# Top-32 attention feeding a squared-ReLU MLP: weights cast by GpSimd DMAs, a reordered first load, and identity products on TensorE

## The chip, the cores and the metric

The kernel runs on one NeuronCore of a Trainium2 chip. The core's engines are TensorE (PE, with its weight loads shown as PEld), VectorE (DVE), ScalarE (ACT), GpSimd (POOL) and SyncE (SP, which here only issues DMAs). The metric is the device time of one execution in microseconds, as the median of several runs. One further execution was taken with the hardware profiler; it has its own time and its own span, from the first instruction to the last.

## The reference

Attention in which each query keeps only its 32 largest scores, followed by a two-layer MLP with a squared ReLU. q, k and v are 8 batches x 8 heads x 576 rows x 64, in fp32.

```python
scores = scale * np.matmul(q, k.transpose(0, 1, 3, 2))
kth = np.partition(scores, -top_k, axis=-1)[..., -top_k:-top_k + 1]
scores = np.where(scores >= kth, scores, -1000000000.0)
attn = softmax(scores)                       # over the last axis
x = np.matmul(attn, v)                       # -> (4608, 512), heads side by side
h = x @ w_in                                 # w_in  512 x 2048, fp32
r = np.maximum(h, 0.0)
out = (r * r) @ w_out                        # w_out 2048 x 512, fp32
```

## The kernel before

**Groups.** The work is cut into 144 groups, 18 for each batch: a group is 128 query rows of two heads (a "pair" of heads shares one load), or, for the last 64 rows of a head (`Z`), 64 rows of four heads. In batches 0 to 6 the order is first row blocks 0 and 1 of each pair, then blocks 2 and 3 with the `Z` groups between them; in the last batch it is `Z`, then blocks 2 and 3, then block 0 of all pairs and block 1 of all pairs.

**One group.** `top_k` (L519) makes the scores on PE: eight fp32 matmuls into `ps_s`, three PSUM banks of which there is one set only. ACT copies them to SBUF (`s`, L555). DVE forms maxima of halves (`pairs`, L611, which read `ps_s` and so release it for the next scores); one of the two goes to a PSUM bank `ps_q`, and ACT copies it into `m` (L619). DVE combines the two (L621), and POOL forms the lower values by whole-number additions and subtractions (L606). Then DVE takes eight maxima at a time and strikes them out: MAX8 (L638) and MATCH_REPLACE8 (L642) on 104, 124 and 272 columns for each of the two halves, and one MAX8 over all 576 (`kth`, L645). The strikes wait for POOL's operation `mid`. ACT makes the mask term `w` from scores and threshold (L653).

`attend` (L669) transposes the scores on PE and adds the mask with a product by `steep_bf`; the ninth block of it uses the bank `ps_q` too. ACT takes the exponential into `p` (L687). `collect` multiplies by v, ACT copies the result (`av`, L714), DVE takes reciprocals (L716), POOL scales (`x`, L718), PE transposes and ACT copies into `xt` or `xz` (L742, L743). When all heads of 256 rows are there, `feed` (L748) runs the MLP on that chunk: products with `win`, ReLU on ACT (L768), square on POOL or ACT (L782, L785; on DVE for the last chunk, L779), products with `wo`, a copy (`o`, L802) and the store (L810).

**Loads.** `load_pair` (L459) issues three DMAs for q (`rq`), three for k (`rk`) and five for v (`rv`); the first pair's k goes out on ACT's queue, everything else on SP's. PE transposes q and k through `ident32`, ACT copies them into `qk` (L511 to L514), POOL casts v (L515).

**Weights.** `setup` (L856) makes the identities and constants on POOL, and then brings in the two weight matrices in 16 pieces of 0.5 MB of fp32: a DMA on SP's queue into one of two staging buffers `ws`, which lie in the last slots of the MLP's own buffer `g`, and a cast into `win` or `wo` on ACT or POOL (L894). The pieces with `i % 4` of 0 or 1 go to ACT, eight in all, and the others to POOL.

```python
pl.op("sp", 4.0, WD * i - 60, lambda ...: [nc.sync.dma_start(view(s), src)],
      w=[s], take=[s], ndma=1, sem=..., nbf=WN)
eng, fn = ("act", act.copy) if i % 4 < WA else ("gp", gp.tensor_copy)
weights.append(pl.op(eng, 1.1, WC * i, lambda ...: fn(dst, view(s)), r=[s]))
```

**What sets the order.** Nothing is ordered by hand. Each operation is given to a `Plan` with an engine, an estimated duration and a priority (smaller goes first), and `Plan.schedule` (L120) plays the program through with these durations: at each moment an idle engine takes its ready operation of the smallest priority whose buffers are free. An operation is not ready before its `nbf` time. The order that comes out is emitted for each engine and is fixed: at run time every engine works in that order, waiting on semaphores. Priorities are due times: group n (from 0) has `tg = T0 + PER * n` with `T0 = 12.0` and `PER = 5.55`. Named constants shift them: `LEAD` (scores), `ME` and `MQ` (the pair operations and their combination), `MA`, `MP`, `TW` (mask), `TA`, `TL` and `NL` (`attend`, with an extra lead that grows over the last `NL` groups up to `TL`), `LAG`, `STEP` and, for the last batch, `LAGL` (`feed`).

Of the kernel before, what the change touches and what calls it, by code (L numbers as in the profile page):

```python
# [8 lines left out]
FP32 = mybir.dt.float32  # L9
# [3 lines left out]
P = 128  # L13
# [63 lines left out]
class Op:  # L77
    __slots__ = ("eng", "dur", "prio", "fn", "deps", "tiles", "takes", "n", "users", "start", "end",
                 "idx", "sem", "val", "ndma", "seq", "vc", "waits", "wars", "later", "nbf", "lk", "late",
                 "via")  # L80
# [5 lines left out]
class Plan:  # L86
# [3 lines left out]
    def op(self, eng, dur, prio, fn, r=(), w=(), u=(), hold=(), take=(), after=(), order=(), sem=None, ndma=0, nbf=0.0, lk=False, late=0.0, via=None):  # L90
# [6 lines left out]
        o.sem, o.ndma, o.seq, o.nbf, o.lk, o.late, o.via = sem, ndma, len(self.ops), nbf, lk, late, via  # L97
# [22 lines left out]
    def schedule(self, t0=0.0, latency=0.12, own=0.07):  # L120
# [24 lines left out]
        while events:  # L145
# [19 lines left out]
            for e in ENGS:  # L165
# [3 lines left out]
                while ready[e]:  # L169
# [23 lines left out]
                    hold = o.dur if e != "sp" else 0.6 * o.ndma  # L193
                    o.end = o.start + o.dur + (hold if e == "sp" else 0)
# [15 lines left out]
class Emitter:  # L210
# [9 lines left out]
    def number(self, plan):  # L220
        for e in ENGS:
            for o in plan.order[e]:
                if e == "sp":
# [12 lines left out]
        seq = sorted(plan.ops, key=lambda o: (o.start, 0 if o.eng != "sp" else 1, o.seq))  # L236
# [41 lines left out]
    def emit(self, plan, e, eng):  # L278
        for o in plan.order[e]:
# [5 lines left out]
            if e == "sp":  # L285
                for i in ins:
                    i.then_inc(self.sem(o.idx[0]), 16)
            else:
                ins.then_inc(self.sems[e], 1)


def bass_top_k_attn__then__act_relu_squared_kernel(
# [22 lines left out]
    def sb(name, shape, dt=FP32, n=None):  # L315
# [7 lines left out]
    ME = 16.41  # L323
    MQ = 15.52
    MP = 18.0
    MA = 18.98
    SQ = 5.15
    TA = 7.2
    TW = -0.14
    TL = 8.0  # L330
    NL = 28.07
    WD = 3.33
    WC = 1.75
    WA = 1.13
    WN = 6
    NBO = 3.81
    LAG = 11.28
    STEP = 3.19
    LATE = 2.38
    LAGL = 11.07  # L340
# [21 lines left out]
        "rq": ([P, 5, 2, D], FP32, 2), "rk": ([P, 5, 2, D], FP32, 2), "rv": ([P, 12, D], FP32, 2),  # L362
# [9 lines left out]

# [3 lines left out]
    NWS = 2  # L376
    mem["ws"] = [gmem[:, NG - 4 - 4 * i:NG - 4 * i, :].rearrange("p a c -> p (a c)").bitcast(FP32) for i in range(NWS)]
    pools["g"], pools["ws"] = Pool("g", NG), Pool("ws", NWS)
# [70 lines left out]
    first_h = []  # L449

    def build(full, weights, pl):
# [6 lines left out]

        def load_pair(b, hp, base):  # L459
# [3 lines left out]
            def load(t, src, rest, queue=nc.sync):  # L463
                def fn():
                    r = at(t)
                    res = []
                    for h in range(2):
                        r0 = 64 if h and rest != (512, 512) else 0
                        res.append(queue.dma_start(r[:, 0:4, h, :], src[b, 2 * hp + h, r0:r0 + 512, :].rearrange(
                            "(tb p) d -> p tb d", p=P)))  # L470
                    x = src[b, 2 * hp, rest[0]:rest[0] + 64, :]
                    res.append(queue.dma_start(r[0:64, 4, :, :], bass.AP(
# [13 lines left out]
            pl.op("sp", 2.3, base - 80, load(rq, q, (512, 512)), w=[rq], take=[rq], sem=slot_sem, ndma=3)  # L486
            via = "act" if not full and not state["pairs"] else None
# [260 lines left out]
        def feed(chunk, xt, tm, step):  # L748
# [7 lines left out]
            for i, g in enumerate(gs):  # L756
# [18 lines left out]
                if chunk in FIRST and weights:  # L775
                    first_h.append(ho)
# [224 lines left out]
```

## Time and profile before

| | |
|---|---|
| median of 3 runs | 872.97 us (872.86 to 874.77) |
| the profiled execution: time | 870.8 us |
| the profiled execution: span | 869.0 us |
| DVE busy | 822.5 us (95%) |
| PE busy | 809.9 us (93%) |
| POOL busy | 788.2 us (91%) |
| ACT busy | 760.3 us (87%) |
| moved by DMA | 48.21 MB, mean 55 GB/s |
| first DVE instruction | 12.51 us |
| last cast of weights | 71.81 us |

The page gives busy times over the whole span and a row of 40 slices for each engine, where a digit is the busy share in tenths. A table of stages gives the same for stretches that the reader picks. The view of waits says for each group of instructions what the engine stood idle for, in total, how often, and the longest. The timeline lists instructions in order of time, with the idle time just ahead of them and what ended it in brackets. A matmul's end is modelled, so a busy PE is not a PE at its peak rate.

### The profile page before, as it was taken

To read this page: it belongs to the slowest core of one execution; us is meant where nothing else is said; L and a number is where in the kernel's file an instruction comes from. 1 tells how busy PE (TensorE), PEld (TensorE's weight loads), DVE (VectorE), ACT (ScalarE), POOL (GpSimd) and SP (SyncE) were. 2 spreads that over 40 slices of the span, in tenths; PEclk is the share of its full clock that TensorE was granted. 3 is DMA by queue.
4 is the path that set the end of the run, shared out by engine and by line. 5 is a ranking of instruction groups with operands and counts; after the bars stand their busy time and mean duration, and the time that the engine had idled before them with its cause. 6 is when DMAs were issued, how large, how long until landed. Compare 5 with 4: busy or idle time off the path is not lost.

```text
span 869.0 us, 22447 instructions
## 1 busy us (share of the span) xinstructions
PE 809.9 (93%) x7911; PEld 612.7 (71%) x7970; DVE 822.5 (95%) x3413; ACT 760.3 (87%) x1261; POOL 788.2 (91%) x826
## 2 busy tenths in 40 slices
PE   5777999989999999998999999999999999999996
PEld 3555777757687777766878677777777767677784
DVE  2989999999999999999999999999999999999971
ACT  4787998989898899989989799889999889898973
POOL 6898999999999998999999889998999987999971
PEclk9899999999999999999999999999999999999999
DMA  7881212131210223012131022202121021100000
GB/s 176 210 231 49 56 29 69 28 85 26 55 43 14 67 56 77 21 38 58 29 87 26 25 60 59 74 13 56 44 68 42 14 52 43 41 2 14 26 25 31
DMA packets 126969, 48.21 MB, mean 55 GB/s; under 512 B 119168, under 2 KB 119168, under 8 KB 126848
## 3 DMA queue, kind: packets, MB, share of 16 engines
q1 hardware_dynamic: 125648, 46.39, 21.3%
q8 instruction: 65, 1.06, 0.5%
q14 instruction: 56, 0.46, 0.2%
q10 hardware_dynamic: 1200, 0.30, 0.2%
HBM read 37.22 MB, written 9.44 MB: 54 GB/s over the span
## 4 chain that ended last, share of the span: by engine, by line
DVE 64%; PE 17%; ACT 11%; issue 4%; POOL 1%; DMA 1%; SPq 0%; DVEq 0%
DVE f L642 21%; DVE c L638 16%; PE ps L444 13%; DVE kth L645 13%; DVE f L621 5%; PE ps L447 5%; DVE ps L611 5%; DVE m L611 4%; ACT s L555 3%; ACT p L687 3%; ACT w L653 1%; ACT g L768 1%; POOL f L606 1%; POOL t L606 1%; DVE rzall L716 1%
## 5 line engine op out<-in xcount | busy, mean ns | idle before, releaser
L642 DVE MATCH_REPLACE8 f<-c,f 128x104 f32<-128x104 f32 (+2 forms) x864 | 272.2, 325 | 0.0
L638 DVE MAX8 c<-f 128x8 f32<-128x104 f32 (+2 forms) x864 | 248.8, 329 | 0.0
L447 PE MATMUL ps<-ident,s 128*128 128x128 f32 x1296 | 223.1, 281 | 21.5 <-ACT p L687 14.7
L653 ACT ACTIVATE w<-s,kth 128x576 bf16<-128x576 f32 x288 | 222.8, 786 | 19.8 <-DVE kth L645 18.5
L444 PE MATMUL ps<-qk 64*128 64x64 f32 (+3 forms) x1280 | 214.2, 454 | 10.2 <-DVE m L611 8.8
L606 POOL TENSOR_TENSOR t<-s 128x576 int32<-128x576 int32 x144 | 202.5, 1411 | 13.2 <-ACT s L555 13.1
L645 DVE MAX8 kth<-f 128x8 f32<-128x576 f32 x288 | 209.5, 757 | 0.0
L606 POOL TENSOR_TENSOR f<-t,m 128x576 int32<-128x576 int32 x144 | 203.2, 1411 | 0.1
L444 PEld LDWEIGHTS ps<-qk 64*128 64x128 f32 (+1 forms) x1280 | 132.6, 181 | 86.6 <-issue 62.9
L555 ACT COPY s<-ps 128x1152 f32<-128x1152 f32 x144 | 161.5, 1121 | 34.7 <-PE ps L444 33.7
L447 PEld LDWEIGHTS ps<-ident,s 128*128 128x128 f32 x1296 | 144.3, 142 | 48.0 <-ACT p L687 23.6
L687 ACT ACTIVATE p<-ps 128x1152 bf16<-128x1152 f32 x144 | 163.3, 1134 | 8.7 <-PE ps L444 7.8
L444 PE MATMUL ps<-steep_bf,w 128*128 128x128 bf16 x1296 | 141.1, 220 | 0.0
L606 POOL TENSOR_TENSOR t<-m 128x288 int32<-128x288 int32 x144 | 115.0, 799 | 19.3 <-ACT m L619 14.7
L444 PE MATMUL ps<-wo,g 128*128 128x512 bf16 x517 | 127.9, 379 | 4.0 <-issue 1.1
L444 PE MATMUL ps<-xt,win 128*128 128x256 bf16 (+1 forms) x1152 | 126.6, 261 | 1.5 <-ACT qk L511 0.8
L606 POOL TENSOR_TENSOR f<-t,f 128x288 int32<-128x288 int32 x144 | 114.9, 798 | 0.0
L444 PEld LDWEIGHTS ps<-xt,win 128*128 128x128 bf16 x1152 | 97.9, 98 | 15.9 <-ACT g L768 1.2
L444 PEld LDWEIGHTS ps<-steep_bf,w 128*128 128x128 bf16 x1296 | 106.0, 101 | 4.2
L782 POOL TENSOR_TENSOR g<-g 128x512 bf16<-128x512 bf16 x92 | 95.7, 1042 | 12.9 <-ACT g L768 11.7
L768 ACT ACTIVATE g<-ps 128x512 bf16<-128x512 f32 x144 | 86.0, 606 | 10.1 <-PE ps L444 9.3
L611 DVE TENSOR_TENSOR ps<-ps,s 128x288 f32<-128x288 f32 x144 | 66.6, 462 | 22.1 <-ACT s L555 17.1
(60 smaller groups left out, 882.4 us busy)
## 6 DMA issues: line engine op xcount, KB each, us to landing
rq<-in_q_dram SPq DMA_DIRECT2D x64, 128.0 KB, 2.5
rv<-in_v_dram SPq DMA_DIRECT2D x64, 128.0 KB, 2.4
out_dram<-o SPq DMA_DIRECT2D x32, 256.0 KB, 2.1
rk<-in_k_dram SPq DMA_DIRECT2D x62, 128.0 KB, 2.6
g<-in_moe_w_in_dram SPq DMA_DIRECT2D x8, 512.0 KB, 4.3
g<-in_moe_w_out_dram SPq DMA_DIRECT2D x8, 512.0 KB, 4.3
rv<-in_v_dram SPq DMA_DIRECT2D x96, 16.0 KB, 2.1
rq<-in_q_dram SPq DMA_DIRECT2D x32, 32.0 KB, 2.5
```

The costliest lines, as they stand in the source:

```text
L444: return pe.matmul(o, l, r, start=start, stop=stop, skip_group_check=True)
L447: return pe.matmul(o, i, ident, is_transpose=True, skip_group_check=True, **kw)
L555: cp = [pl.op("act", 1.2, tg - LEAD + 1, lambda: act.copy(at(st)[:, :, :], two(banks(ss), SECOND, S)), r=[ss], w=[st])]
L606: return pl.op("gp", dur, prio, lambda: gp.tensor_tensor(o().bitcast(I32), x().bitcast(I32), y().bitcast(I32), op), **kw)
L611: return vec.tensor_tensor(o, two(banks(ss)[:, a:], SECOND + HALF, QUART), two(at(st)[:, 0, HALF + a:], HALF, QUART), ALU.max)
L638: lambda i=i, t=t, c0=c0, c1=c1: vec.max(eighth(t, i), at(f)[:, i, c0:c1]),
L642: lambda i=i, t=t, c0=c0, c1=c1: vec.match_replace(at(f)[:, i, c0:c1], eighth(t, i), at(f)[:, i, c0:c1], NEG), hold=[f])]
L645: ks.append(chain(kth, i, prev[i] + [low], .665, lambda i=i: vec.max(eighth(kth, i), at(f)[:, i, :]), hold=[f]))
L653: pl.op("act", .77, tw + .8 * i, lambda i=i: act.activation(at(wt)[:, i, :], at(st)[:, i, :], ACTF.Relu, bias=kth[:, i, n:n + 1], scale=-1.0),
L687: pl.op("act", 1.15, tt + 1, lambda: act.activation(at(pt)[:, :, :].rearrange("p k q -> p (k q)"), banks(e)[:, 0:2 * S], ACTF.Exp, scale=0 ...
L768: return act.activation(at(g)[:, 0:kf * nt], bank(hh)[:, 0:kf * nt], ACTF.Relu)
L782: pl.op("gp", .15 + w_ / 480, tf + lag + 1, lambda g=g: gp.tensor_tensor(at(g)[:, 0:w_], at(g)[:, 0:w_], at(g)[:, 0:w_], ALU.mult), u=[g])
```

## The change

Four things change.

- **Weights.** The staging buffers and the 16 casts go. Eight DMAs of 1 MB of fp32 are issued by POOL and write bf16 straight into `win` and `wo`. They have a high priority on POOL and are not ready before `6 + 6.19 * i` us in the plan. `feed` waits for pieces of the new size.
- **The first pair.** k of the first head goes out on ACT's queue and k of the second on SP's; of q only the first 128 rows of both heads are loaded next, and the rest after that, into a third `rq` buffer. PE transposes the first block of q and all of k, DVE (not ACT) copies most of k into `qk`, and the rest of q is transposed and copied after the first group's scores have been planned.
- **Identity products.** PE gets products of `ident_bf` with itself, 128x512 into a PSUM bank, whose results nobody reads: 36 of them 0.22 us apart in the plan from 0 to 8 us, and 51 more 1.2 us apart up to 70 us. Their priority is the lowest, so that the plan puts them where PE has nothing else that is ready; each takes one of the two `psum` buffers.
- **The plan's constants and its model of DMAs** (a `bw` term holds the queue for the time that a load takes).

```diff
@@ Plan.schedule
-                    hold = o.dur if e != "sp" else 0.6 * o.ndma
-                    o.end = o.start + o.dur + (hold if e == "sp" else 0)
+                    hold = o.dur if e != "sp" else max(o.bw, 0.6 * o.ndma * (o.via is None))
+                    o.end = o.start + o.dur + (hold if e == "sp" else o.bw)
@@ constants
-    ME = 16.41
-    MQ = 15.52
+    ME = 21.85
+    MQ = 19.61
-    MA = 18.98
-    SQ = 5.15
+    MA = 18.27
+    SQ = 5.7
-    TW = -0.14
-    TL = 8.0
-    NL = 28.07
-    WD = 3.33
+    TW = -1.88
+    TL = 19.68
+    WARM = 8
+    WP = 6.19
+    BW = 1
+    WSTEP = 1.2
+    WEND = 70
+    NL = 6.65
-    LAG = 11.28
-    STEP = 3.19
-    LATE = 2.38
-    LAGL = 11.07
+    LAG = 12.79
+    STEP = 2.98
+    LATE = 1.39
+    LAGL = 20.8
@@ buffers
-        "rq": ([P, 5, 2, D], FP32, 2), ...
+        "rq": ([P, 5, 2, D], FP32, 3), ...
-    NWS = 2
-    mem["ws"] = [gmem[:, NG - 4 - 4 * i:NG - 4 * i, :]... for i in range(NWS)]
@@ build
+        def load_first(b, hp, rq, rq2, rk, base):
...
+            pl.op("sp", .1, base - 82, start(nc.scalar, lambda: part(rk, k, 0, 0, 4),
+                                             lambda: rest(rk, k, REST[0], REST[1] - REST[0])),
+                  w=[rk], take=[rk], sem=slot_sem, ndma=2, via="act")
+            pl.op("sp", 2.3, base - 81, start(nc.sync, lambda: part(rk, k, 1, 0, 4)), w=[rk], sem=lambda o: "first", ndma=1)
+            pl.op("sp", 2.3, base - 80, start(nc.sync, lambda: (at(rq)[:, 0, :, :], both)), w=[rq], take=[rq],
+                  sem=slot_sem, ndma=1)
+            pl.op("sp", 2.3, base - 79, start(
+                nc.sync, lambda: part(rq2, q, 0, 1, 3), lambda: part(rq2, q, 1, 1, 3), lambda: rest(rq2, q, 512, 0)),
+                w=[rq2], take=[rq2], sem=slot_sem, ndma=3)
+
+        def first_pair(rq, rq2, rk, rv, qk, vb, base):
...
+            o_x = pl.op("pe", .15, base - 45.2, flips(tx, rq, [0]), r=[rq], w=[tx], take=[tx, qk])
+            o_k = pl.op("pe", .5, base - 45.1, flips(tk, rk, [0, 1, 2, 3]), r=[rk], w=[tk], take=[tk], order=[o_x])
...
+            pl.op("act", .3, base - 42.5, lambda: act.copy(at(qk)[:, 0:128], bank(tx)[:, 0:128]), r=[tx], w=[qk])
+            pl.op("dve", .6, base - 42.5, lambda: vec.tensor_copy(at(qk)[:, 640:1152], bank(tk)), r=[tk], w=[qk])
...
@@ setup
-        for i in range(16):
-            s = tile("ws")
...
-            weights.append(pl.op(eng, 1.1, WC * i, lambda s=s, dst=dst, view=view, fn=fn: fn(dst, view(s)), r=[s]))
+        for i in range(8):
+            if i < 4:
+                half, c2 = divmod(i, 2)
+                src = wi[:, 2 * c2:2 * c2 + 2, 1024 * half:1024 * half + 1024]
+                dst = win[:, 2 * c2:2 * c2 + 2, 1024 * half:1024 * half + 1024]
+            else:
+                src, dst = wo_ap[:, 4 * i - 16:4 * i - 12, :], wo[:, 4 * i - 16:4 * i - 12, :]
+            weights.append(pl.op("gp", 1.0, WC * i - 60, lambda src=src, dst=dst: [gp.dma_start(dst, src)], ndma=1,
+                                 sem=lambda o, i=i: f"w{i}", nbf=WN + WP * i, bw=7.0))
+
+        times = [.22 * i for i in range(int(WARM / .22))]
+        times += [WARM + WSTEP * i for i in range(int((WEND - WARM) / WSTEP))]
+        for x in times:
+            t = Tile(psum)
+            pl.op("pe", .22, 1e5, lambda t=t: mm(bank(t), ident_bf[:, :], ident_bf[:, :].unsqueeze(1).broadcast_to(
+                [P, 4, P]), True), w=[t], take=[t], after=[i2], nbf=x)
```

## The prediction

> **What bounds the kernel now.** I read the slices of the page, then a table of stages, then VectorE's (DVE's) waits, then the timeline where DVE stands still.
>
> ```profile
> PE 809.9 (93%) x7911; PEld 612.7 (71%) x7970; DVE 822.5 (95%) x3413; ACT 760.3 (87%) x1261; POOL 788.2 (91%) x826
> DVE  2989999999999999999999999999999999999971
> ```
>
> ```profile
> 0.00:12.50 12.50, 4.84 (x18) 3.44 (x18) 0.00 (x0) 3.86 (x6) 5.11 (x31) 1.00 0.85 183
> 12.50:30.00 17.50, 13.88 (x60) 10.18 (x60) 12.55 (x50) 10.71 (x19) 14.14 (x14) 1.00 0.78 192
> 30.00:65.00 35.00, 25.94 (x208) 20.29 (x207) 31.99 (x132) 29.24 (x44) 32.33 (x33) 0.85 0.87 222
> 65.00:90.00 25.00, 19.13 (x176) 13.92 (x173) 23.23 (x96) 19.50 (x32) 21.83 (x23) 0.93 0.22 62
> 90.00:840.00 750.00, 724.37 (x7214) 548.93 (x7268) 748.92 (x3123) 684.23 (x1138) 709.20 (x720) 1.00 0.17 43
> 840.60:862.20 21.60, 21.13 (x241) 15.44 (x242) 5.07 (x16) 11.67 (x24) 5.61 (x8) 1.00 0.07 26
> ```
>
> The columns are PE, PEld, DVE, ACT and POOL busy, granted clock, DMA share, GB/s. From 90 to 840 us DVE is busy 748.92 of 750: the middle is DVE-bound and cannot shrink unless DVE work does. What can be won lies at the ends: 12.5 us before DVE starts, 4.95 idle from 12.5 to 30, 3.0 to 65, 1.8 to 90, and 28.4 after the last threshold (its MAX8 pair ends at 840.6), where PE is busy 21.13 of 21.6.
>
> ```profile
> DVE ps L611 <- ACT s L555: 17.1, 4, 12.5
> DVE ps L611 <- ACT p L687: 4.8, 6, 1.3
> ```
>
> ```profile
> 5.91 1.09 PE L447 MATMUL ps<-ident,rq 128*128 128x128 f32 x4 [5.91 <-DMA rq<-in_q_dram]
> 8.81 2.50 PE L444 MATMUL ps<-qk 64*128 64x64 f32 x8 [0.56 <-ACT qk L514]
> 11.36 1.12 ACT L555 COPY s<-ps 128x1152 f32<-128x1152 f32 x1 [2.60 <-PE ps L444]
> 12.51 0.47 DVE L611 TENSOR_TENSOR ps<-ps,s 128x288 f32<-128x288 f32 x1 [12.51 <-ACT s L555]
> 17.09 0.47 DVE L611 TENSOR_TENSOR ps<-ps,s 128x288 f32<-128x288 f32 x1 [2.72 <-ACT s L555]
> 30.12 1.34 PE L444 MATMUL ps<-qk 64*128 64x64 f32 x8
> 35.86 1.06 PE L447 MATMUL ps<-ident,rk 128*128 128x128 f32 x4
> 71.20 2.47 PE L444 MATMUL ps<-qk 64*128 64x64 f32 x8
> ```
>
> DVE's early waits are for score copies (17.1 us, 12.5 of it the start) and then for the exponential (4.8). One set of eight score matmuls takes 2.50 us until 29 us and 1.34 at 30.12: PE runs at about half pace at first, though the clock column prints 1.00 there. It falls back from 35.83 to 42.65, 56.30 to 59.72 and 69.96 to 73.37 (granted 0.50 to 0.52), each time after about 3.4 us in which PE was busy only 1.25, 1.52 or 0.77. The rise at 29 follows 3.4 us with PE busy 3.32.
>
> **The change, part by part.**
>
> *Start.* Before, the first transposes wait for 288 KB of q beside 288 KB of k (5.91). After, 352 KB come first: k and 128 rows of q. The 2.50:5.00 stretch moved 243 GB/s, so I estimate these landed near 4.7. But identity products stand ahead. `ident_bf` is ready at 2.0; reading the planner's rules, its times put the first q at 3.6, so ten products of 0.22 precede the first transpose in PE's in-order program. The nearest row, 16 matmuls of 128x512 bf16 in 3.40 us, gives 0.22 each at full pace, and 1.85 times that (2.50/1.35) 0.41 cold: ten end at about 6.3. That, not the DMA, sets the first transpose. PE is then dense from 2.1 on, which by the 29 us rise lifts the clock within two 3.4 us stretches, 5.5 to 8.9. From 6.3: one transpose of q, four of k, one of the rest, 0.9 to 1.0; a DVE copy of 512 columns, 0.6 (ACT's L511 takes 0.59); scores from 7.9, 1.35 if warm; the L555 copy 1.12; DVE at 10.6. Against 12.51 that is -1.9 (+0.5 if all stays cold, -3.5 if the products take less). The DVE copy itself costs nothing: DVE has no other work then.
>
> *Two queues.* The trace gives 3.8 us to landing for k's 128 KB on ACT's queue against SP's median 2.5 to 2.6. The Trainium skill (DMA: Bandwidth & Descriptors, Issuing engines are not separate DMA queues) says DMAs from different engines share 16 engines and only issue time is saved; here that is one SP issue, 0.5 us. By row or by rule the sum is the same zero while the products end at 6.3; with that cover gone, 0.5 to 1.3. ACT's two issues end before its 1.28 us table load is due.
>
> *Ramp to 30.* Pairs of group 1 to pairs of group 2 is 4.58 us, with 2.87 idle. Warm scores take 1.15 off: idle 1.7. The other 2.1 (0.94, 0.88 and smaller) are shorter than 1.15 each and go. 4.95 becomes 1.7: -3.2 (0 if cold). What is late next is GpSimd: its two low-half operations (1.39 and 0.79) release the first MATCH_REPLACE, about 15.0.
>
> *Ramp 30 to 90.* The 4.8 idle wait for L687 while ACT is busy 29.24 of 35 and PE goes cold three times. Removing eight ACT casts (8 x 1.05 = 8.4 us) and much of the cold pace helps both. I take half, -2.5 (0 to -4.8). The 51 later products (0.22 each, 11.2 us) have the lowest rank and fill PE's idle: 3.6+9.1+5.9 = 18.6 us. Without that cover each holds the matmul behind it by at most 0.22 (0.41 cold). They also take one of two PSUM slots, so PE can wait at one for a late ACT copy; I cost that at 0 to 1. They do not assure the clock: three of them in a stretch with 0.77 busy make 1.43, under the 1.52 after which it fell.
>
> *Weights.* POOL loses eight casts (8.3 us) and gets eight DMA instructions. No row shows a DMA issued by GpSimd. Nearest is SP's issue of half the size, 0.59, so 1.2 for 1 MB; the bounds are 0.34 (SP's shortest) and 3.1. Sum 9.6, 1.3 more than the casts, against POOL idle of 3.4+2.7 = 6.0 us from 12.5 to 65: 0. Queued behind each are the L606 operations, and DVE's MATCH_REPLACE waits for those. SP loses 16 issues. Buffer waits disappear (5.4 us on ACT's casts, and more), so loads of q, k and v are issued earlier. The 8 MB read are unchanged. Transfers now interleave with pair loads; DMA share was already 0.87 from 30 to 65, one k load cost PE 1.3, and I allow 0 to 3. Lateness of the weights themselves costs nothing until the first activations are complete (last L742 copy of batch 0's first tile at 101.3); the last cast was at 71.8 before, the last issue is due at 49.3 now.
>
> The upper bound of 3.1 comes from a rule against this change. The trace's POOL operations hold 1.407 us in the first 90 us and 1.411 overall, so DVE's operations do not block them. The Trainium skill (SBUF — State Buffer, Who interferes with whom and the box on the SWDGE trap) says GpSimd cannot write descriptors while DVE holds the shared port in a two-port mode, 0.62 us becoming 3.1; it lists copies, casts and tensor_scalar from SBUF to SBUF. DVE's rows here are MAX8, MATCH_REPLACE8 and TENSOR_TENSOR from PSUM, and the added copy reads PSUM. By the row the sum stays; by the rule, if it applied, 8 x 3.1 - 8.3 - 6.0 = 10.5 us come back. I take the row.
>
> *Planner constants.* Earlier pair operations, longer feed lags: no instruction is added. In the middle DVE has no gap to close, so 0 at best, up to +4 if a buffer runs out (six score buffers, three of m). At the end the last groups' transposes rank up to 19.7 us earlier and the last feeds later. The trace shows x waiting behind POOL's squares (exponential at 848.0, x at 853.22), but PE has 0.5 idle in 21.6, so order alone wins 0.5: -0.5 (-3 to +3).
>
> **Sum.** -1.9 - 3.2 - 2.5 - 0.5 = -8.1. Span 869.0 to 860.9; the profiled execution took 870.8, 1.8 around the span, so 862.7. The median shown, 872.97, is 2.2 above it: 864.9.
>
> **The rivals.**
>
> *Little of the ramp is PE's* (0.14). The products only push the transposes back and the clock rises as late as before; half of the 30 to 90 gaps go with the casts: -2.5, 870.5. For it: 0.83-busy stretches (35.83 to 39.24) did not lift the clock. Against: ten products leave no hole.
>
> *GpSimd becomes the bound in the ramp* (0.13), the slower side. Each DMA instruction holds POOL for d; 8d - 8.3 - 6.0 reaches the path. At d = 2.8 the 8.1 gain is gone; at 4.0 it is +9.6, 882.6; at 3.1, 875.4. For it: POOL is 92% busy from 30 to 65 and DVE waits for it within every group. Against: the rows above.
>
> *The new leads and lags open gaps* (0.10). 0.03 us in each of 130 groups and 3 in the tail are 7: -1, 872. For it: PE is 97% busy and in order. Against: no view shows a buffer at its limit in the middle.
>
> **How the numbers follow.** The first case has 0.63, its own range 860 to 869, all faster. About 0.3% (2.6 us) is what a measurement of this kernel can tell from no change. Faster: 0.63, half of the PE case, 0.04 of the last, 0.74. Slower: 0.11 of GpSimd's and 0.03 of the last, 0.14. Same: 0.12. The range 858.5 to 874 leaves out most of GpSimd's case and some 0.05 below.
>
> **What would show it.** Right: first DVE pairs near 10.6, first scores at 1.35, DVE idle between there and 90 under 5, DMA rows on POOL near 1.2, last threshold near 832. Wrong: score sets of 2.5 after 10 us, POOL rows over 2.8, new gaps after 90, or a stretch from last threshold to end above 31.

## The result and the profile after

The changed kernel takes 871.98 us (median, 871.24 to 872.66), the kernel before 872.91 beside it: a ratio of 0.9987 with a 95% interval of 0.9968 to 1.0007. That is no difference that can be told apart; 864.9 was forecast. The profiled execution of the changed kernel took 872.66 us, its span is 870.8. The profiled execution of the kernel before (span 869.0, mean granted clock 0.990) was a quick one: of the 150 fast executions of that kernel that ran beside the experiments, 56 with a granted clock of 0.988 or more have a median of 870.7 us and the other 94 one of 873.7, so a difference between these two profiles is nearly 3 us less favourable than one between medians. All four executions of the changed kernel had 0.996 or more, and a median of 871.98: its higher clock did not become time.

The page of the changed kernel, busy times and VectorE's slices:

```profile
PE 826.5 (95%) x8002; PEld 609.3 (70%) x8057; DVE 827.1 (95%) x3414; ACT 755.1 (87%) x1250; POOL 789.3 (91%) x829
...
DVE  3899999999999999999999999999999999999981
```

The table of stages of the changed kernel, with the columns as before (PE, PEld, DVE, ACT and POOL busy, granted clock, DMA share, GB/s):

```profile
0.00:12.50 12.50, 9.50 (x33) 3.50 (x33) 2.11 (x5) 3.73 (x7) 6.65 (x33) 1.00 0.83 157
12.50:30.00 17.50, 16.79 (x99) 9.33 (x98) 13.39 (x56) 9.55 (x18) 15.85 (x18) 1.00 0.85 155
30.00:65.00 35.00, 31.02 (x230) 19.90 (x230) 31.47 (x130) 25.72 (x41) 28.98 (x31) 0.95 0.99 167
65.00:90.00 25.00, 22.46 (x226) 16.17 (x224) 24.37 (x100) 21.38 (x35) 23.42 (x23) 1.00 0.12 26
90.00:840.00 750.00, 722.47 (x7158) 543.18 (x7206) 747.63 (x3105) 680.95 (x1127) 706.74 (x719) 1.00 0.17 43
840.00:862.00 22.00, 21.35 (x258) 16.11 (x260) 7.79 (x23) 13.22 (x25) 7.66 (x10) 1.00 0.07 25
```

The start did what the change says: the clock is up (0.95 and 1.00 where it was 0.85 and 0.93), and VectorE has 2.11 us of work before 12.5 us where it had none. From 30 to 90 us it is hardly busier than before. And from 840 us on it still has 7.79 us to do, where it had 5.07 in nearly the same stretch: it came to the end later, not earlier.

To see this exactly I counted, for every VectorE instruction, the time from its start to the next start, less what is usual for its kind. The rest is lost time, also the part too short for the view of waits. What is called usual moves all rows of a kind together, so the differences are firmer than the levels.

| lost by VectorE, us | before | after | difference | forecast |
|---|---|---|---|---|
| until the first pair operation | 12.5 | 10.9 | -1.6 | -1.9 |
| from there to 30 us | 5.7 | 4.9 | -0.9 | -3.2 |
| 30 to 90 us | 6.0 | 5.5 | -0.6 | -2.5 |
| 90 us to the last threshold | 10.4 | 15.0 | +4.7 | 0 |
| last threshold ends at | 840.6 | 842.3 | +1.7 | 832 |
| from there to the end of the span | 28.4 | 28.6 | +0.2 | -0.5 |

The start of the changed kernel in its timeline:

```profile
2.06 3.17 PE L444 MATMUL ps<-ident_bf 128*128 128x512 bf16 x7 [2.06 <-POOL ident_bf L921]
5.02 0.42 PE L447 MATMUL ps<-ident,rq 128*128 128x128 f32 x1
5.29 1.27 PE L444 MATMUL ps<-ident_bf 128*128 128x512 bf16 x2
6.62 0.86 PE L447 MATMUL ps<-ident,rk 128*128 128x128 f32 x5
7.32 0.69 DVE L500 COPY qk<-ps 128x512 f32<-128x512 f32 x1 [7.32 <-PE ps L447]
8.38 1.34 PE L444 MATMUL ps<-qk 64*128 64x64 f32 x8
9.78 1.12 ACT L616 COPY s<-ps 128x1152 f32<-128x1152 f32 x1 [1.77 <-PE ps L444]
10.34 3.09 PE L444 MATMUL ps<-ident_bf 128*128 128x512 bf16 x8
10.94 0.47 DVE L672 TENSOR_TENSOR ps<-ps,s 128x288 f32<-128x288 f32 x1 [2.93 <-ACT s L616]
13.36 1.35 PE L444 MATMUL ps<-qk 64*128 64x64 f32 x8
15.91 0.47 DVE L672 TENSOR_TENSOR ps<-ps,s 128x288 f32<-128x288 f32 x1 [3.12 <-ACT s L616]
```

The first scores take 1.34 us: the clock is warm by 8.4, as forecast, and the first pair operation stands at 10.94 (10.6 forecast). Group 2's scores could have started when the pair operations of group 1 let the bank go, at 11.76. They start at 13.36, because eight products (3.09 us) stand ahead of them. So VectorE waits 3.12 us again at 15.91, where 1.7 was forecast. VectorE's waits to 90 us in the changed kernel are still mostly for that copy:

```profile
DVE ps L672 <- ACT s L616: 8.4, 4, 3.1
DVE qk L500 <- PE ps L447: 7.3, 1, 7.3
DVE ps L672 <- ACT p L748: 1.7, 3, 1.0
```

GpSimd's part is quickly told. Its DMA instructions, from 0 to 90 us, by group (busy us, mean ns):

```profile
L948 POOL DMA_DIRECT2D wo<-in_moe_w_out_dram x4 | 3.1, 782 | 0.0
L948 POOL DMA_DIRECT2D win<-in_moe_w_in_dram x4 | 3.1, 773 | 0.0
```

That is 6.2 us in place of 8.3 of casts: GpSimd did not become the bound.

### The profile page after: what moved, and what is told of

The parts are those of the page before. It is cut to its first block, busy times and chain, and to the rows that moved or that the text cites. A ratio compares the mean times of both kernels' runs of the same rounds, so it can differ in the third digit from the quotient of the medians.

```text
span 870.8 us, 22557 instructions
## 1 busy us (share of the span) xinstructions
PE 826.5 (95%) x8002; PEld 609.3 (70%) x8057; DVE 827.1 (95%) x3414; ACT 755.1 (87%) x1250; POOL 789.3 (91%) x829
## 4 chain that ended last, share of the span: by engine, by line
DVE 75%; PE 12%; ACT 5%; issue 3%; POOL 3%; DMA 1%; SPq 1%; DVEq 0%; POOLq 0%
DVE f L703 24%; DVE c L699 18%; DVE kth L706 16%; PE ps L444 9%; DVE f L682 5%; DVE ps L672 5%; DVE m L672 5%; PE ps L447 3%; ACT p L748 2%; ACT s L616 1%; ACT w L714 1%; POOL t L667 1%; POOL f L667 1%; ACT g L829 1%; DMA rq<-in_q_dram 1%
## 5 line engine op out<-in xcount | busy, mean ns | idle before, releaser
L703 DVE MATCH_REPLACE8 f<-c,f 128x104 f32<-128x104 f32 (+2 forms) x864 | 267.6, 317 | 0.0
L699 DVE MAX8 c<-f 128x8 f32<-128x104 f32 (+2 forms) x864 | 244.7, 321 | 0.0
L444 PE MATMUL ps<-qk 64*128 64x64 f32 (+3 forms) x1280 | 208.1, 443 | 2.9 <-DVE m L672 2.7
L444 PEld LDWEIGHTS ps<-qk 64*128 64x128 f32 (+1 forms) x1280 | 128.7, 176 | 78.4 <-issue 65.9
L841 POOL TENSOR_TENSOR g<-g 128x512 bf16<-128x512 bf16 x95 | 98.6, 1042 | 11.6 <-ACT g L829 10.7
L444 PEld LDWEIGHTS ps<-wo,g 128*128 128x128 bf16 x576 | 51.4, 98 | 48.9 <-ACT qk L575 0.9
```

The source lines that it names most:

```text
L444: return pe.matmul(o, l, r, start=start, stop=stop, skip_group_check=True)
L699: lambda i=i, t=t, c0=c0, c1=c1: vec.max(eighth(t, i), at(f)[:, i, c0:c1]),
L703: lambda i=i, t=t, c0=c0, c1=c1: vec.match_replace(at(f)[:, i, c0:c1], eighth(t, i), at(f)[:, i, c0:c1], NEG), hold=[f])]
L841: pl.op("gp", .15 + w_ / 480, tf + lag + 1, lambda g=g: gp.tensor_tensor(at(g)[:, 0:w_], at(g)[:, 0:w_], at(g)[:, 0:w_], ALU.mult), u=[g])
```

## The experiments

Ratios are to the kernel before, measured on the same chip beside each; in brackets the 95% interval. The changed kernel has 0.9987 on this scale. "Lead" is by how much VectorE finishes a group's threshold sooner than in the profile of before.

### Which part costs the middle: constants and products

My first theory was that the new leads (`ME`, `MQ`, `MA`) cost the middle. Ahead of the combination (L682), which waits for ACT's copy of `m`, 4.6 us were lost after 90 us, where it had been 0.5.

```diff
-    MA = 18.27        # m copy due earlier
+    MA = 24.42
```

> The changed kernel with one constant moved: MA from 18.27 to 24.42, so that ACT's copy of m is due 2.6 us ahead of the pair operations, as in the kernel before, and not 3.6 us behind them. Theory 1 (the new leads cost the middle: DVE's combination L682 is ordered right behind a copy of m that ACT now serves late, 4.6 us of short stalls after 90 us): the stalls go, the last threshold ends 4 to 5 us earlier, about 867.5 us. Rival (the middle is slower for another reason, such as a different order of the DVE operations): 871 to 873.

Measured: 873.35, 1.0009 [0.9992, 1.0026]. Missed: the loss ahead of L682 went from 4.6 to 4.0 only, others rose, the middle lost 19.0 us in all and the last threshold ended at 844.1.

```diff
-        for x in times:
+        times = []            # no identity products
+        for x in times:
```

> The changed kernel without any of the 87 identity products. Theory 2 (the products give a faster PE early, but stand ahead of needed matmuls in its fixed order and give as much back): within 2 us of the changed kernel, 870 to 874, with cold score sets of 2.5 us and first pairs near 11. Rival (the products carry the ramp, and the loss is all elsewhere): 4 to 6 us slower, 876 to 878.

Measured: 875.02, 1.0027 [1.0005, 1.0049], between the two.

```diff
-    WEND = 70
+    WEND = 8              # only the first 36 products
```

> The changed kernel with the first 36 products alone; the 51 later ones are gone. Theory 2: the standstill of 30 to 37 us, where six products hold k's transposes back by about 2.2 us, shrinks; 1 to 2 us faster, 870 to 871. Rival (the later products keep the clock up and that is worth more): 1 to 3 us slower, 873 to 875.

Measured: 873.65, 1.0017 [0.9993, 1.0041], on the rival's side but not clear.

All 13 constants as before, beginning with:

```diff
-    ME = 21.85
-    MQ = 19.61
+    ME = 16.41
+    MQ = 15.52
```

> The changed kernel with all thirteen planner constants that both kernels have set back to those before (ME, MQ, MP, MA, SQ, TA, TW, TL, NL, LAG, STEP, LATE, LAGL); loads, weights and products stay as changed. Theory 1: stalls after 90 us fall back from 15.0 to about 10.4 as I count them, 867 to 868, or 868 to 869 if the new tail constants had won 0.5 to 1. Rival (the parts in the first 90 us have used up their own gain, and the constants do nothing): 871 to 873.

Measured: 871.16, 0.9982 [0.9962, 1.0001]. The last threshold came 4.5 us sooner than in the changed kernel (837.7), as theory 1 has it, and the middle lost 11.8 us. But the time hardly moved: it is in the rival's range. Then only `ME`, `MQ` and `MA` (18.98) as before:

> The changed kernel with the leads of the pair operations, their combination and the m copy (ME, MQ, MA) as before; the constants of the tail (TL, NL, LAGL, LAG, STEP) stay the new ones. With all constants as before, the last threshold came 4.5 us earlier and the time was 871.16. Theory 1 (the new leads cost VectorE 3 to 4.6 us in the middle, and the end is TensorE's): last threshold near 838 to 839.5, stretch behind it 30 to 32, time 869.5 to 871.5. Theory 2 (VectorE's last threshold plus the new tail's 28.4): 867 to 868.5. If the middle is not the leads' doing, last threshold 842 and 872 to 873.

Measured: 873.34, 1.0018 [1.0001, 1.0035]; last threshold 840.1, middle 14.9; the time is nearest to the last of the three cases. The loss ahead of L682 shrank to 1.3 us, and 5.4 us stand ahead of the pair operations instead. By stretches, against the kernel before: the changed kernel loses 5.3 us more from 90 to 680 us and 0.4 more from 680 to 780, this run 1.6 and 3.6. So the leads do cost in the changed kernel's order, but not by themselves: what their return wins up to 680 us comes back as another wait in the last batch, and a run below that has the new leads and `LAG` moved by 0.5 loses only 2.1 more up to 680 us. And an earlier last threshold does not bring an earlier end.

### What sets the end

In the run with all constants as before, and in the changed kernel, the last mask (`w`) and exponential (`p`) in ACT's timeline; first all constants as before:

```profile
838.49 0.80 ACT L714 ACTIVATE w<-s,kth 128x576 bf16<-128x576 f32 x1
...
846.88 1.13 ACT L748 ACTIVATE p<-ps 128x1152 bf16<-128x1152 f32 x1 [0.60 <-PE ps L444]
```

and the changed kernel:

```profile
843.13 0.78 ACT L714 ACTIVATE w<-s,kth 128x576 bf16<-128x576 f32 x1
...
848.54 1.13 ACT L748 ACTIVATE p<-ps 128x1152 bf16<-128x1152 f32 x1 [1.26 <-PE ps L444]
```

With the old constants the mask is there 4.6 us sooner, the exponential starts 1.7 us sooner. Between the two lies TensorE, which with the old constants reaches the last masked transposes only at 846 and is busy 8.80 of the 8.80 us from 838.0 to 846.8:

```profile
845.82 0.63 PE L447 MATMUL ps<-ident,s 128*128 128x128 f32 x4
846.28 0.39 PE L444 MATMUL ps<-steep_bf,w 128*128 128x128 bf16 x4
```

So I took work away near the end, from VectorE, from TensorE, and from both.

```diff
-    eighth(kth, i), at(f)[:, i, :])
+    eighth(kth, i), at(f)[:, i, 0:HALF if n >= 130 else S])
```

> The changed kernel, with 8 us of VectorE's work left out near the end: in groups 130 to 143 the last MAX8 of each half reads 288 of the 576 columns (14 groups x 2 x 0.30 us = 8.4 us; the thresholds of these groups are therefore taken over half of the columns). The plan and the order are unchanged. Theory 1 (the end is TensorE's: in the last 45 us it stands in an unbroken row, and the last groups' masked transposes run 4 to 12 us after their masks were there): the last threshold comes 7 to 8.4 us earlier, near 834.5, and the stretch behind it grows from 28.4 to 34 us or more; the time falls by no more than 2.5, to 869.5 to 872. Theory 2 (the end is VectorE's last threshold plus a fixed tail): the stretch stays at 28 to 29.5 and the time falls by 7 to 8, to 864 to 865.

```diff
-    for o, c, start in outs:            # mask products
+    for o, c, start in outs[-1:] if n >= 122 else outs:
```

> The changed kernel, with some 7 us of TensorE's work left out near the end: in groups 122 to 143 only the last mask product of each of the three steps is made, 3 of 9 (22 groups x 6 x 0.055 us = 7.3 us; the masks of the other blocks of these groups are therefore not applied). The plan and the order are unchanged. Theory 1 (the end is TensorE's): the time falls by 4.5 to 7.5, to 864.5 to 867.5, while the last threshold stays within 1.5 us of 842.4. Theory 2 (the end is VectorE's last threshold plus a fixed tail): only the products behind the last threshold count (two groups, 0.7 us), 871 to 872.5.

> The changed kernel with both pieces of work left out together: VectorE's 8.4 us (the last MAX8 of groups 130 to 143 reads 288 of 576 columns, so these thresholds come from half of them) and TensorE's 7.3 us (in groups 122 to 143 three of nine mask products are made). Alone, the first took 2.4 us off the profiled span and the second 2.2, and each left the relieved engine waiting for the other. Theory 1 (VectorE and TensorE are equally full and release each other in a fixed order, so that relief of one goes over into waits for the other): together they give more than the sum of the two, 6 to 8.5 off the span of 870.8, 862.3 to 864.8, and a time of 863.5 to 866. Theory 2 (something else sets the end, GpSimd with 39 of 40 us busy from 780 to 820, or the order of the last feeds): no more than the sum, 866 to 868.5 of span, a time of 867 to 870.

| work left out | time | ratio | last threshold | span |
|---|---|---|---|---|
| none (changed kernel) | 871.98 | 0.9987 | 842.3 | 870.8 |
| VectorE 8.4 us | 870.29 | 0.9971 [0.9955, 0.9987] | 838.5 | 868.4 |
| TensorE 7.3 us | 871.28 | 0.9995 [0.9978, 1.0012] | 840.3 | 868.6 |
| both | 866.80 | 0.9937 [0.9921, 0.9954] | 836.0 | 865.1 |

The stage from 780 to 840 us, in the order: nothing, VectorE's, TensorE's, both left out (first number behind the length is PE, third DVE):

```profile
780.00:840.00 60.00, 58.32 (x639) 44.80 (x641) 60.00 (x257) 52.42 (x92) 58.08 (x64) 1.00 0.06 19
```

```profile
780.00:840.00 60.00, 59.16 (x660) 46.17 (x664) 56.71 (x263) 53.10 (x94) 58.30 (x64) 1.00 0.06 19
```

```profile
780.00:840.00 60.00, 55.84 (x572) 40.71 (x578) 60.00 (x259) 52.42 (x93) 57.15 (x62) 1.00 0.06 19
```

```profile
780.00:840.00 60.00, 58.34 (x606) 42.60 (x607) 57.24 (x258) 54.21 (x96) 58.40 (x64) 1.00 0.06 19
```

VectorE, relieved of 8.4 us, idles 3.3 of 60 (0 before) and ends 3.8 sooner, not 8.4. TensorE, relieved of 7.3, idles 4.2 (1.7 before) and VectorE stays full. By the ratios the first is worth 0.16% against the changed kernel, the second nothing, both together 0.50%, 4.4 us; of the span 2.4, 2.2 and 5.7. Not all of the span's difference is the edits': at group 120, ahead of any work left out, VectorE already stood 0.9, 1.4 and 2.5 us ahead of the changed kernel's profile, which the edits cannot have brought about. Without that, 1.5, 0.8 and 3.2 of the span remain.

By its time the first run is in theory 1's range and the second in theory 2's; as the two theories exclude each other, both are too simple: neither engine sets the end alone. They are equally full, each works in a fixed order, and each waits for the other's results; that relief of one becomes its wait for the other is how I read the idle time above. For the pair, 866.8 lies between the ranges of both theories. By the ratios it is more than the sum of the two, though not far outside what the four intervals allow together, and only about a third of the 15.7 us left out. What holds the rest (GpSimd is busy for 57 to 58 of these 60 us in all four) was not tried.

The three runs also show that the loss in the middle goes with the order: from 90 to 680 us, where they still do what the changed kernel does, in the same order, they lost 6.7, 5.3 and 5.3 us more than the kernel before, and the changed kernel 5.3.

### Each part alone

```diff
+    load_first(b, hp, rq, rq2, rk, base)      # first pair alone, in the kernel before
```

> The kernel before, with the change's first-pair loading alone: k of the first pair on two queues, the first block of q ahead of the rest, the copy of k on VectorE; staged weights, no identity products, constants as before. No product stands ahead of the transposes, so these wait for 352 KB: the first transpose near 4.7, all cold; scores 2.5 instead of 1.35: first pair operation near 11.3 against 12.5 before, and the ramp behind it as before. Theory 1 (the end is TensorE's, and the start reaches it only where TensorE starts its dense work earlier): time down by 0 to 1.2, 872 to 873.2. Theory 2 (all of the start is passed on): down by 1.2 to 2, near 871.5.

Measured: 873.1, 1.0005 [0.9993, 1.0018]. First pair operation 10.5 (12.5 before), last threshold 0.7 us sooner, last `o` copy 2.5 later: theory 1, the start is not passed on.

The products alone (the loop over `times` of the change's diff, added to `setup` of the kernel before):

> The kernel before with the identity products alone (87 of 128x512, at the change's times); staged weights, first pair and constants as before. Leaving them out of the changed kernel cost 3 us (875.02 against 872). They stand ahead of the first transposes, which in this kernel wait for 576 KB anyway (5.91 us). Theory 1 (a warm clock from 6.5 us on, paid for with 0.45 us each where TensorE has other work): first pair operation near 11, VectorE's stalls to 90 us 9 to 11 against 11.75, last threshold 1.5 to 3 us earlier; the time, behind a TensorE that is full at the end, 0 to 2 us lower, 871 to 873. Theory 2 (the products are worth all of the ramp): 868 to 870. If they only take TensorE's time: 874 to 876.

Measured: 876.01, 1.0027 [1.0007, 1.0047], the third case at its edge. The first pair operation comes at 14.7, 2.2 later than before. Its timeline shows the price of a product, 0.43 us each at the cold clock:

```profile
2.06 5.70 PE L447 MATMUL ps<-ident_bf 128*128 128x512 bf16 x13 [2.06 <-POOL ident_bf L863]
...
7.58 0.62 PE L450 MATMUL ps<-ident,rq 128*128 128x128 f32 x4
...
8.04 1.94 PE L447 MATMUL ps<-ident_bf 128*128 128x512 bf16 x6
...
9.82 0.66 PE L450 MATMUL ps<-ident,rk 128*128 128x128 f32 x4
```

Thirteen products are ahead of q's transposes, six more ahead of k's. First pair and products together, weights staged:

> The kernel before with the first-pair loading and the identity products, constants as before; the weights stay staged. With the weights as well it was 871.16, with the first pair alone 873.1, with the products alone 876.0. Theory 1 (the start belongs to these two, the weights hardly count): first pair operation 10.6 to 11.3, stalls to 90 us 9 to 11, last threshold 838 to 840, time 870.5 to 873. Theory 2 (eight copies on ACT and their buffers in the ramp were a limit): stalls from 30 to 90 us 6 or more against 4.1 with the weights, time 873.5 to 876.

Measured: 874.86, 1.0030 [1.0010, 1.0049]; stalls from 30 to 90 us 8.9, last threshold 842.2. Theory 2's side.

Products of 128x128 in place of 128x512, all constants as before:

```diff
-    mm(bank(t), ident_bf[:, :], ident_bf[:, :].unsqueeze(1).broadcast_to([P, 4, P]), True)
+    mm(bank(t)[:, 0:P], ident_bf[:, :], ident_bf[:, :], True)
```

> The changed kernel with all constants as before, and with identity products of 128x128 instead of 128x512 (same number, same places in the order). With 128x512 the time was 871.16, the idle time of VectorE to 30 us 4.85, from 30 to 65 us 3.8. Theory 1 (the products hold TensorE twice as long as planned, 0.45 us each, and so eat part of the ramp): group 2's scores come 1.2 to 1.6 us earlier, VectorE's stalls to 65 us fall from 8.7 to 5 to 6.5, and TensorE stays at full clock; last threshold 836, time 868.5 to 870.5. Theory 2 (the products' time is what keeps the clock up): one or more stretches of 3.4 us at half clock come back before 65 us, stalls at 8.7 or more, time 871 to 874.

Measured: 873.59, 1.0002 [0.9985, 1.0018]. Theory 2. The start with the narrow products: k's transposes begin at 4.82, when k has landed, and not at 6.62, but the scores are cold.

```profile
2.06 1.33 PE L444 MATMUL ps<-ident_bf 128*128 128x128 bf16 x7 [2.06 <-POOL ident_bf L921]
...
4.82 1.39 PE L447 MATMUL ps<-ident,rk 128*128 128x128 f32 x5 [0.66 <-DMA rk<-in_k_dram]
...
6.91 2.50 PE L444 MATMUL ps<-qk 64*128 64x64 f32 x8
```

The stages from 30 us with 128x512, then with 128x128:

```profile
30.00:65.00 35.00, 31.00 (x239) 19.56 (x239) 31.93 (x133) 27.18 (x43) 29.34 (x32) 1.00 0.97 167
65.00:90.00 25.00, 22.33 (x226) 16.41 (x225) 25.00 (x100) 21.06 (x35) 24.48 (x24) 1.00 0.11 26
```

```profile
30.00:65.00 35.00, 29.06 (x241) 21.82 (x240) 32.58 (x136) 26.90 (x42) 30.07 (x33) 0.92 0.95 164
65.00:90.00 25.00, 21.50 (x199) 15.37 (x197) 22.84 (x95) 18.97 (x30) 22.08 (x22) 0.91 0.13 28
```

The clock falls to 0.92 and 0.91 again, and over the whole span the twelve executions have 0.988 to 0.993 with the narrow products and 0.994 to 0.999 with the wide ones: the time that a product holds TensorE is what keeps the clock up, and also what delays the work behind it.

The weights alone (the eight `gp.dma_start` of the change's diff in the kernel before, in place of `ws` and the casts):

> The kernel before with the weights alone changed: eight casting DMAs of 1 MB issued by GpSimd instead of 16 staged loads and 16 copies; no identity products, first pair and constants as before. GpSimd's instructions take 0.72 to 0.94 us each, 6.2 in place of 8.3, and ACT loses 8.4 us of copies, all before 72 us. Theory 1 (the copies were hidden in the ramp, because VectorE waited there for scores at a cold clock): stalls from 30 to 90 us fall by no more than 1.5 from 6.0, time 0 to 1.5 lower, 871.5 to 873. Theory 2 (ACT and GpSimd were the ramp's limit, as forecast with -2.5): stalls from 30 to 90 down by 2.5 or more, time 869 to 871.

Measured: 882.84, 1.0115 [1.0093, 1.0136], ten us slower, which neither theory had. VectorE is 2.9 us behind at group 3 and 10 at group 140. The same, with a plan that counts how long a load of q, k or v holds the queue:

```diff
-    BW = 0
+    BW = 1
```

> The kernel before with the weights alone, as in the run of 882.84, but with the plan counting what a load of q, k or v holds of the queue (1.9 us), as the changed kernel does. Theory 1 (transfers of 1 MB meet the pair loads, which the plan did not expect; VectorE lost 3 us by group 3): the loss by group 3 falls to under 1.5 and the time to 874 to 878. Theory 2 (without products TensorE is cold in the ramp, and the order that follows is a bad one): group 3 as late as in that run, 878 to 885.

Measured: 874.93, 1.0030 [1.0012, 1.0048]; 1.5 us behind at group 3, 1.8 ahead at group 12: theory 1's range. The tables of both show the first 1 MB transfers beside the pair loads (DMA share 1.17 and 1.16, clock down), and behind them a hole that only the first has; first the plan without the term, then with it:

```profile
20.00:30.00 10.00, 7.36 (x26) 4.90 (x26) 8.39 (x33) 5.17 (x10) 7.90 (x10) 0.52 1.17 208
...
90.00:110.00 20.00, 17.99 (x160) 14.09 (x161) 17.12 (x71) 16.17 (x29) 16.32 (x17) 0.83 0.14 32
```

```profile
20.00:30.00 10.00, 7.51 (x30) 5.11 (x31) 9.00 (x33) 6.03 (x11) 8.59 (x11) 0.64 1.16 206
...
90.00:110.00 20.00, 19.05 (x192) 14.68 (x192) 20.00 (x80) 19.05 (x34) 19.08 (x20) 1.00 0.08 19
```

No operation differs between these two runs; the eight us between them lie in the order, and so also in when the loads are issued.

### What a new order is worth

No part alone was faster (the first pair the same, the products and the weights slower), and all together are the same. What every variant has in common is another order from the planner. So one constant was moved by half a microsecond, in the kernel before, in the changed kernel, and in the changed kernel with the constants of before; and the 13 new constants were put into the kernel before.

```diff
-    LAG = 11.28
+    LAG = 11.78
```

> The kernel before with one constant moved: LAG (how long after its rows the MLP of a chunk is due) 11.28 to 11.78. No operation is added or removed, and the first 25 us are as before; the planner's order changes from the first feed on in a large part of TensorE's lines. Theory 1 (any new order costs or wins a few us, because TensorE and VectorE are both full and release each other): the last threshold or the stretch behind it moves by 1.5 us or more, the time leaves 873 by 1.5 to 6, more likely upwards, 874 to 879. Theory 2 (only what the parts add and remove counts): 872.3 to 873.8.

> The kernel before with the change's 13 constants alone. Against the changed kernel with all constants as before, the new ones cost VectorE 3 us behind 90 us and won 2 to 3 in the stretch behind the last threshold. Theory 1 (the constants carry that loss with them): stalls behind 90 us 13 to 16 instead of 10.4, time 874 to 877. Theory 2 (they fit only the order that they were drawn up with, and in another are like any other new order): 870 to 882, without that sign; a middle no worse than before's 10.4 would show it.

> The changed kernel with LAG 12.79 moved to 13.29 and nothing else; the first 25 us are as in the changed kernel. Theory 1 (both kernels stand in an order that fits them, and any other costs a few us): 873.5 to 878 against 872, the last threshold or the stretch behind it later by 1.5 or more. Theory 2 (only the kernel before had a lucky order; the changed one is ordinary): 869.5 to 873.

> The changed kernel with all 13 constants as before, and LAG 11.28 moved to 11.78; without the shift it was 871.16, the lowest of all so far that compute everything. Theory 1 (that order was a fitting one, like the one before): 872.5 to 878. Theory 2 (the parts are worth 2 us in any order): 869.5 to 872.5.

| kernel | time | ratio | lead at group 12 | lost after 90 us | last threshold ends | last `o` copy starts |
|---|---|---|---|---|---|---|
| before | 872.91 | 1 | 0 | 10.4 | 840.6 | 862.1 |
| before, `LAG` + 0.5 | 877.48 | 1.0057 [1.0036, 1.0078] | 1.5 | 13.5 | 842.2 | 866.9 |
| before, new constants | 876.14 | 1.0037 [1.0020, 1.0054] | 4.0 | 15.5 | 841.9 | 864.2 |
| changed | 871.98 | 0.9987 [0.9968, 1.0007] | 3.2 | 15.0 | 842.3 | 864.5 |
| changed, `LAG` + 0.5 | 874.29 | 1.0030 [1.0014, 1.0046] | 5.7 | 13.7 | 838.4 | 864.2 |
| changed, old constants | 871.16 | 0.9982 [0.9962, 1.0001] | 4.4 | 11.8 | 837.7 | 862.7 |
| the same, `LAG` + 0.5 | 872.07 | 1.0016 [0.9997, 1.0035] | 5.4 | 14.8 | 839.8 | 863.4 |

The last four columns are of one profiled execution each; that of the new constants in the kernel before took 872.6 us, 3.5 under its median.

Shifting one due time by 0.5 us cost the kernel before 0.57%, with no operation changed: half of it in VectorE's middle (+3.1), half behind the last threshold (+3.2). A lower clock is not the cause: executions with a granted clock of 0.988 or more have a median of 870.7 in the kernel before, 875.7 (five) with `LAG` shifted and 876.1 (eight) with the new constants. The changed kernel lost 0.4% by the same shift, although its last threshold came 3.9 us sooner. Theory 1 of the first, second and third run holds in its numbers. The second's does not hold as a cause: the old constants with `LAG` shifted lose 14.8 us after 90 us too, so the loss goes with the order and not with the new constants alone. For the last run the time is in theory 2's range, but its ratio rose from 0.9982 to 1.0016. No version beats both kernels clearly; the lowest that computes everything is the changed one with the old constants, 871.16.

So the order that the kernel before stands in is worth some 4 us against the two others that were tried (0.57% and 0.37%); that every variant gave this up is an inference. An estimate of what the parts are worth: the changed kernel in five orders other than its own (1.0009, 1.0018, 1.0030, 0.9982, 1.0016) has a mean of 1.0011; the kernel before in two others (1.0057, 1.0037) 1.0047. The difference is 0.36%, 3 us; with each kernel's own order counted in it is 0.24%, 2 us. From so few orders that is rough.

## Why the prediction was wrong

The step that failed is *Planner constants* together with the tail: nothing was allowed for a middle that loses, and the middle lost 4.7 us. The ramp to 30 us was mis-sized beside it, by 2.3. Term by term:

*Start, -1.9.* Right: -1.6. TensorE met the first block of q at 5.0 behind seven products of 0.43 (ten of 0.41 were forecast), k at 6.6 behind two more, and the scores, behind the tenth, took 1.34.

*Two queues, 0.* Right: k's 128 KB landed 2.9 us after their issue on ACT's queue, and the products stood ahead of k's transposes.

*Ramp to 30, -3.2.* Mis-sized: -0.9. The clock came up as forecast. But a product was costed at 0.22 us at full pace, and five of the eight at 10.34 follow each other at 0.45 (all eight take 3.09). And the prediction let the later products cost the work behind each "at most 0.22 (0.41 cold)"; eight in a row ahead of group 2's scores cost 1.6.

*30 to 90, -2.5.* In this profile -0.6, but in five other runs with the same start (`MA` moved, leads as before, `LAG` moved, VectorE's work left out, both left out) VectorE lost 3.0 us there, 3.0 less than before. The term was right for those. The profiled execution of the changed kernel had two things that they have not. Some 0.8 us were lost between 50 and 70 us, with a stretch at a lower clock from 60 to 65 (0.66). Some 1.6 us lie between 30 and 40 at full clock, where TensorE stands still for a load of q:

```profile
31.57 0.63 PE L447 MATMUL ps<-ident,rq 128*128 128x128 f32 x4 [1.41 <-DMA rq<-in_q_dram]
```

The run with TensorE's work left out has the same order and the same wait, no fall of the clock, and lost 4.5 us from 30 to 90. That is the prediction's "allow 0 to 3" for transfers beside pair loads: in both runs these loads of q were issued around a 1 MB transfer at 23.3 to 23.9 us, and in the run with VectorE's work left out, which does not wait, they were issued by 22.4, ahead of it. With the term the start and the ramp gave 5 to 5.5 us in those five runs, of 7.6 forecast; the lead at group 12 says the same (5.2 to 5.7, against 3.2 in the changed kernel's profile).

*Weights.* GpSimd's instructions at 0.78 us mean lie under the 1.2 that I took, and far under 3.1: the row decided rightly. The stretching from 0.62 to 3.1 us of which the Trainium skill warns (SBUF — State Buffer, A bandwidth-pool intuition that's wrong) is that of a whole DMA beside a VectorE copy, so as a bound for GpSimd's instruction it was my own estimate; no instruction here took more than 0.94, with VectorE's MAX8 and MATCH_REPLACE8 as neighbours. In the run with the weights alone VectorE was 2.9 us behind by group 3.

*Constants, 0, and the tail, -0.5.* Here the step failed. I read "busy 748.92 of 750" as a middle that cannot shrink and so will not grow ("up to +4" was allowed only for a buffer that runs out, and went into the sum as nothing), and counted every microsecond won at the start as won at the end. The middle lost 4.7 us more, of which the busy time shows only 1.3 as idle (747.63 for 748.92); that is 0.036 us for each of 130 groups, the size in the rival of the new leads, which named 872 and was given 0.10. Its cause, the leads, holds only in part: their return won 3.7 us up to 680 us and lost 3.2 in the next 100. And where the middle kept the lead (837.7 and 838.4 for the last threshold), the stretch behind it grew by 3 to 4 us: TensorE, in its own order, arrives when it arrives. I had seen it 97% busy and called VectorE the bound.

*The sum.* A sum of edits supposes that the rest stays as it is. Here every edit makes the planner draw up another order, and the kernel before stood in one that fits about 4 us better than the two others that were tried. That term was missing, and it is as large as the parts' own gain (2 to 5.5 us).

## What to carry to other kernels

Where two engines are 97 and almost 100% busy in fixed orders, a gain at the start is kept only if both come through the middle and the end with it: look at both engines' arrival at the end, not at the busy share of one. Where a planner draws up the order from constants tuned to it, first move a constant by a little and see what a new order alone does; a forecast smaller than that scatter is not worth making, and a part tried alone in the old constants is judged by its order more than by its work. Filler work is costed by how long it holds its engine, measured one behind the other in the buffers that it will have, and by its place ahead of the first real work.

## What was not expected of the hardware

- Products that nobody reads follow each other at 0.43 us while cold. At full clock some rows have 0.22 to 0.23 from one to the next, as in the feeds, and others 0.45, where the next weight load stands idle until the product ahead is done. Two rows of the changed kernel at full clock, and a weight load of the first:

```profile
10.34 3.09 PE L444 MATMUL ps<-ident_bf 128*128 128x512 bf16 x8
...
28.88 1.28 PE L444 MATMUL ps<-ident_bf 128*128 128x512 bf16 x5
...
11.24 0.10 PEld L444 LDWEIGHTS ps<-ident_bf 128*128 128x128 bf16 x1 [0.35 <-PE ps L444]
```

  The first row stands behind transposes of q, which in the plan hold one of the two `psum` buffers until they are copied; the products then all go into the other, and each is made to wait for the one ahead. That is read from the kernel and the row; no run gave the products another buffer.

- A casting DMA of 1 MB (512 KB written) costs GpSimd 0.72 to 0.94 us and takes 6.8 us from issue to landing (median in the changed kernel), 6.1 to 6.2 in the run with the weights alone.
- Nine products between 2 and 6.6 us have the clock up by 8.4 us, where it had come up at 29; with the same products at a quarter of the width the first scores still take 2.50. When it comes up without products differs between executions: with `LAG` shifted in the kernel before, whose first 25 us are planned as before, the scores at 18.91 took 1.35, and those at 22.46 again 2.50.
